# Reordering the two sides of TensorE's interleaved steps: a lone maximum first, two scores next, dense halves from the second pair

## The chip, the cores and the metric

The kernel runs on one core of one Trainium2 chip. The metric is the device time in microseconds of one launch. Differences are taken against the kernel before, whose median over three runs is 1616.48 us.

## What is computed

The input `x` has 2048 rows of 512. It is normalised row by row, and two branches read the result. One is attention with 32 heads of width 16 that share one key and one value head. The other is a dense layer to 1792, the Mish activation, and a dense layer back to 512. The second branch goes through SiLU and gates the first, and `x` is added:

```
xn = layernorm(x)
q = xn @ wq   (32 heads of 16);  k = xn @ wk;  v = xn @ wv   (one head of 16)
s = softmax(q k^T / 4) v, heads joined, @ wo
h = xn @ w1 + b1;  g = silu((h * tanh(softplus(h))) @ w2)
out = x + s * g
```

## The kernel before, in words

The attention is cut into 32 units `v` (a block of 512 queries and four heads) of 16 steps `s`, which makes 512 steps. In one step TensorE produces:

- four score tiles (`e`, line 875), each 128 keys by 512 queries, contracted over 64 rows of the array. ScalarE turns each into `pt` with an exponential (line 877). Score tiles rotate through three PSUM banks.
- four maximum tiles (`m`, line 895), which are the scores of a later unit with queries in the partitions. VectorE reduces each to its row maximum (line 899), from which the softmax shift of that unit is made. They rotate through three other banks.
- four pairs of value products (`pv`, line 949) of the step before the last. They use all 128 rows of the array, with four outputs side by side, and they close the step.
- some dense work (`xps`, line 109): a share of one of the matmul groups of the projections and of the dense branch, in the single bank that is left for it.

**Halves and pairs.** A matmul that contracts over 64 rows uses half of the array, so two of them on different halves run side by side. A score or maximum tile is such a matmul by nature. A dense matmul contracts over 128 rows and is cut into two halves that add into the same bank. In step `s`, the dense side is the row half `h = s % 2` and the other is the score side. `waves` builds both lists and issues them alternately, one dense-side matmul and one score-side matmul at a time. A chunk of `k` dense matmuls has its first halves in one step and its second halves in the next, since `h` alternates. `XMAX = 8` is the largest chunk. A group of 12 dense matmuls makes two chunks of six and so four steps. A group of 15 makes a chunk of eight and one of seven. Here these are called six-half, seven-half and eight-half steps. Counted along the trace, the stretch in which `waves` runs holds 358 six-half steps, 58 of each of the others, and 12 steps without dense work.

**Who gets the maxima.** `m_sides(1 - h, k // 2)` gives the score side `n` of the four maxima, so that both sides come out about equally long: three in six- and seven-half steps, four in eight-half steps. What is left, one lone maximum in six- and seven-half steps, goes to the dense side. `EM = "MEMEMEME"` is the order of the score side; a letter for a maximum that the side doesn't have is skipped. In a six-half step the order before is therefore, pair by pair and dense side first: x|M, x|E, x|M, x|E, x|M, x|E, M|E.

**Two waits of a dense chunk.** The second halves must not run into the bank ahead of the first ones. `waves` therefore remembers, as `relay`, the consumer of the first score-side tile that is issued after the last half (an exponential on ScalarE or a reduction on VectorE), and makes the first half of the next step wait for it. In the last step of a group no relay is needed: the group's `post` is issued right after the last half. It reads the bank out ("evacuates" it) on ScalarE (`hb` line 652 for the first dense layer, `qf` line 593 for the query projection, `y` line 717 for the first third of the second dense layer) or on VectorE (`y` lines 721 and 153, for the other two thirds and the output projection). The next group's first half waits for this evacuation, as there is one bank. For a group that VectorE evacuates, maxima that are issued between the last half but one and the last one are put on VectorE's queue behind the evacuation (`HOLD`, `held`).

The order of instructions on each engine is what this program order says: each engine works through its own queue in order. Waits of second order (buffer reuse) are inserted by the framework. Where an instruction needs two waits, one of them becomes an instruction of its own in front of it.

At the end of each step come the jobs of the activation chain on ScalarE (`act_jobs`, at most one or two), then the value products. The steps of the beginning are laid out by a planner and those of the end by `fill`; neither uses the lines that the change touches.

Of the kernel before, what the change touches and what calls it, by code (L numbers as in the profile page):

```python
# [41 lines left out]
STEP_US = 2.95  # L42
XMAX = 8
NPT = 14
EM = "MEMEMEME"
MLAG = 4
NHB = 3
NACT = 7
# [11 lines left out]
def m_need(v):  # L60

    return (40, 64)[v] if v < 2 else 32 * (v + 1)
# [53 lines left out]
def block_kernel(ctx: ExitStack, tc: tile.TileContext, x, wq, wk, wv, wo, w1, b1, w2, out):  # L116
# [232 lines left out]
    def act_jobs(n):  # L349
        n = (int(len(jobs) > 2) if gap[0] else n) if n < 9 else n  # L350
        gap[0] = 0
        while n > 0:
            k = next((k for k, (fn, free) in enumerate(jobs)
                      if free is None or free() is not None and free() <= step[0]), None)
            if k is None:
                return
            fn = jobs[k][0]
            del jobs[k]
            fn()
            n -= 1  # L360
            ran[0] += 1
# [84 lines left out]
    def pump():  # L446
        for tag in items:
            while arrived(tag):
                split(tag)
            load(tag)  # L450
# [14 lines left out]
    def begin():  # L465
        prepare()
        if qqueue and is_ready(qqueue[0]):
            g = qqueue.popleft()
        elif queue and is_ready(queue[0]):
            g = queue.popleft()  # L470
        else:
            n = next((n for n, g in enumerate(queue) if g.wo is None), None)
            if not n or not is_ready(queue[n]) or queue[n].m1 is None:
                return False
            g = queue[n]
            del queue[n]
        if g.start:
            g.start()
        if g.alloc:
            ps = g.alloc()  # L480
        else:
            ps = ps_x.tile([P, 512], F32, tag="x", name="xps")
        cur.update(g=g, n=0, ps=ps, chunk=[], relay=None)
        return True

    def finish():
        g = cur["g"]
        if cur["n"] < len(g.mms):
            return False
        for i in g.items:  # L490
            i.users -= 1
        cur["g"] = None
        evacs[0] += g.dve
        if lead:
            lead["post"](g, cur["ps"])
        else:
            g.post(cur["ps"])
            g.done = step[0]
        return True
# [14 lines left out]
    def chunk_size(n):  # L514
        return -(-n // -(-n // XMAX)) if n else 0

    def waves(h, em, new):

        if not cur["chunk"] and (not new or cur["g"] is None and not begin()):
            mms = []
        else:
            g = cur["g"]
            mms = cur["chunk"] or g.mms[cur["n"]:cur["n"] + chunk_size(len(g.mms) - cur["n"])]
        second = bool(cur["chunk"])
        k = len(mms)
        ms = em(k)
        a = deque(ms[1 - h])  # L530
        b = deque(ms[h])
        ps = cur["ps"]
        ends = second and cur["n"] + k == len(cur["g"].mms)
        xs = deque(mms)
        relay = None
        first = True
        done = False
        while a or b or xs:
            if xs:
                i = xs.popleft().half(ps, h)  # L540
                if first and cur["relay"] is not None:
                    tc.add_manual_dep(i.ins, cur["relay"].ins.name, mybir.DependencyInfo(
                        mybir.DependencyClass.Sync, mybir.DependencyReason.DATA), reason="other half of the bank")
                first = False
                if ends and cur["g"].dve and len(xs) == HOLD:
                    held[0] = []
                if not xs and ends:
                    cur["n"] += k
                    cur["chunk"] = []
                    finish()  # L550
                    done = True
                    for top in held[0] or ():
                        top()
                    held[0] = None
            elif b:
                b.popleft()()
            if len(a) > 1 or a and not xs:
                r = a.popleft()()
                if k and not xs and relay is None:
                    relay = r  # L560
        if k and not done:
            assert relay is not None
            cur["relay"] = relay
            if second:
                cur["n"] += k
                cur["chunk"] = []
            else:
                cur["chunk"] = mms
# [295 lines left out]
    def e_one(s, i):  # L864

        v, r = divmod(s, 16)
        if s < NS - LEAD:
            a, k, p = 1 - s % 2, r - r % 2 + i // 2, i % 2
        else:
            a, k, p = i % 2, r, i // 2  # L870
        q = qt_of[v]
        o = 64 * a
        ps, tag = (ps_m, "m") if NS - LEAD <= s and i in ((1, 3) if s < NS - 4 else (3,)) else (ps_e, "e")
        e = ps.tile([P, C], F32, tag=tag, name=f"e{s}_{i}")
        pe.matmul(e, ks[o:o + 64, P * k:P * (k + 1)], q[o:o + 64, p], start=True, stop=True)  # L875
        pt = sb.tile([P, C], F32, tag="pt", name=f"pt{s}_{i}", bufs=NPT)
        r = act.activation(pt, e, AF.Exp, scale=0.25)  # L877
        pt_of[16 * v + k, p, a] = pt
        return r
# [24 lines left out]
    def m_sides(h, n):  # L904

        ahead = m_next[h] - m_next[1 - h]
        lo = max((4 - MLAG - ahead + 1) // 2, 4 - (32 * NU - m_next[1 - h]))
        hi = min((4 + MLAG - ahead) // 2, 32 * NU - m_next[h])
        return max(min(n, hi), lo)
# [116 lines left out]
    def due(t):  # L1026
        step[0] = t
        for k in sorted(k for k in timed if k <= t):
            for fn in timed.pop(k):
                fn()  # L1030
# [85 lines left out]
    for c0, c1 in ((0, 1), (1, 2), (2, 4)):  # L1116
# [4 lines left out]
        for c in range(c0, c1):  # L1121
            xs, his = [], []
# [29 lines left out]
            if c == 0:  # L1152
                qp = task("PE", 2.8, lambda: fill(12), xs)
                xs = [qp]
# [33 lines left out]
    def best(eng):  # L1188
        found = None
        for k in plan[eng]:  # L1190
            s = k.start(T[eng])
            if s is not None and (found is None or (max(s, T[eng] + 0.1), k.prio) < (max(found[0], T[eng] + 0.1), found[1].prio)):
                found = (s, k)
        return found
# [5 lines left out]
    while True:  # L1200
# [7 lines left out]
        b = best("PE")  # L1208
# [13 lines left out]
        s, e, k = min(opts, key=lambda o: o[0])  # L1222
# [36 lines left out]
        elif k == "J":  # L1259
            tag = next((g for g in ("wq", "ws", "wb") if arrived(g) and busy[0] + E0 < s + 0.5), None)  # L1260
            n = ran[0]
# [16 lines left out]
    while left:  # L1278
        k = next(k for k in left if all(d.end is not None for d in k.deps))
# [6 lines left out]
    for s in range(NS + 2000):  # L1286
        inm = s < NS - LEAD
        if inm or cur["chunk"]:
            assert s < NS
            due(s)  # L1290
            h = s % 2

            def em(k):
                n = m_sides(1 - h, k // 2) if inm else 0
                x = deque(lambda i=i: e_one(s, i) for i in range(4))
                y = deque(lambda: m_one(1 - h) for _ in range(n))
                r = [[], []]
                for op in EM:
                    if op == "M" and y:
                        r[1 - h].append(y.popleft())  # L1300
                    elif op == "E":
                        r[1 - h].append(x.popleft())
                r[h] = [lambda: m_one(h) for _ in range(4 - n if inm else 0)]
                return r

            if s >= 2 and (s - 1) % 16 == 0 and s > 1:
                gap[0] += 1
            waves(h, em, inm)
            act_jobs(1 + (len(jobs) > 2))
            due(s + 0.5)  # L1310
            if s >= 2:
                pv(s - 2)
                if (s - 1) % 16 == 0 and s > 1:
                    o_out((s - 17) // 16)
        else:
            due(s)
            if s < NS:
                for i in range(4):
                    e_one(s, i)
                fill(4)  # L1320
            act_jobs(2 if s < NS else 100)
            if s < NS + 2:
                pv(s - 2)
                if (s - 1) % 16 == 0:
                    o_out((s - 17) // 16)
            due(s + 0.5)
            if s >= NS:
                fill(16)
        step[0] = s
        if vdone[0] < 8 * NC and min(m_next) >= m_need(vdone[0]):  # L1330
            r = c_rows(vdone[0])
            rowq.extend([r[0], r[1], lambda r=r: (r[2](), r[3]())])
            vdone[0] += 1
        if rowq and not evacs[0]:
            rowq.popleft()()
        evacs[0] = 0
        pump()
        if s > NS + 1 and not queue and cur["g"] is None and not timed and not jobs:
            break
# [12 lines left out]
```

## Time and profile before

| | us |
|---|---|
| median of three runs | 1616.48 (1615.63 to 1619.14) |
| span of the profiled execution, first to last instruction | 1612.9 |
| what lies around the span, taken as the median less the span | 3.6 |
| PE busy | 1594.2 (99%) |
| VectorE busy | 1348.5 (84%) |
| ScalarE busy | 1294.7 (80%) |
| GpSimd busy | 620.8 (38%) |

The page names no other time for the profiled execution than its span, so that row of the table is a difference. In the timeline PE lists matmuls, PEld their weight loads, DVE is VectorE and ACT is ScalarE. Times count from the start of the span. Where a line has "x4", four instructions of one group that follow each other are merged into one line, from the start of the first to the end of the last. A matmul's end is modelled by the profiler; starts are recorded.

### The profile page before, as it was taken

To read this page: it belongs to the slowest core of one execution; us is meant where nothing else is said; L and a number is where in the kernel's file an instruction comes from. 1 tells how busy PE (TensorE), PEld (TensorE's weight loads), DVE (VectorE), ACT (ScalarE), POOL (GpSimd) and SP (SyncE) were. 2 spreads that over 40 slices of the span, in tenths; PEclk is the share of its full clock that TensorE was granted. 3 is DMA by queue.
4 is the path that set the end of the run, shared out by engine and by line. 5 is a ranking of instruction groups with operands and counts; after the bars stand their busy time and mean duration, and the time that the engine had idled before them with its cause. 6 is when DMAs were issued, how large, how long until landed. Compare 5 with 4: busy or idle time off the path is not lost.

```text
span 1612.9 us, 31471 instructions
## 1 busy us (share of the span) xinstructions
PE 1594.2 (99%) x11615; PEld 851.9 (53%) x11615; DVE 1348.5 (84%) x2300; ACT 1294.7 (80%) x2490; POOL 620.8 (38%) x627
## 2 busy tenths in 40 slices
PE   8999999999999999999999999999999999999998
PEld 5455545555555555555555555555555555555534
DVE  8988888888988888888898988888889898888802
ACT  5478788788888778877988787797788878879885
POOL 3875176166265103421524133154153223315522
PEclk9999999999999999999999999999999999999999
DMA  5332133042231304212113321231241313022020
GB/s 161 145 115 64 41 122 111 15 148 83 70 114 52 109 23 153 70 31 91 52 27 111 92 75 26 91 119 38 67 135 34 113 57 96 23 73 78 21 86 26
DMA packets 72776, 127.30 MB, mean 79 GB/s; under 512 B 21488, under 2 KB 34288, under 8 KB 72112
## 3 DMA queue, kind: packets, MB, share of 16 engines
q1 hardware_dynamic: 72624, 125.30, 24.9%
q8 instruction: 92, 1.51, 0.4%
q14 instruction: 60, 0.49, 0.1%
HBM read 76.36 MB, written 27.26 MB: 64 GB/s over the span
## 4 chain that ended last, share of the span: by engine, by line
PE 95%; DVE 2%; ACT 1%; DMA 1%; issue 0%; POOL 0%; SPq 0%; DVEq 0%; ACTq 0%; POOLq 0%
PE xps L109 46%; PE pv L949 31%; PE m L895 8%; PE e L875 5%; PE xps L105 3%; DVE mb L899 1%; PE wop L105 1%; PE warm L1178 0%; PE kp L289 0%; ACT xin L194 0%; DMA xin<-in_dram 0%; DVE st L214 0%; DMA ws<-w 0%; DVE xin L240 0%; PE xp L250 0%
## 5 line engine op out<-in xcount | busy, mean ns | idle before, releaser
L899 DVE TENSOR_REDUCE mb<-m 128x1 f32<-128x512 f32 x2048 | 1272.8, 683 | 184.4 <-PE m L895 157.5
L877 ACT ACTIVATE pt<-e 128x512 f32<-128x512 f32 x2048 | 1068.4, 604 | 253.0 <-PE e L875 236.8
L895 PE MATMUL m<-ks,qt 48*128 48x512 f32 (+1 forms) x2048 | 837.4, 422 | 3.0 <-DVE mb L899 2.5
L875 PE MATMUL e<-qt,ks 64*128 64x512 f32 x2048 | 746.4, 410 | 0.0
L949 PE MATMUL pv<-pt,vaug 128*32 128x512 f32 x4096 | 545.3, 605 | 0.0
L895 PEld LDWEIGHTS m<-ks,qt 48*128 48x128 f32 (+1 forms) x2048 | 370.6, 185 | 67.2 <-DVE mb L899 35.2
L875 PEld LDWEIGHTS e<-qt,ks 64*128 64x128 f32 x2048 | 370.7, 186 | 26.3 <-ACT pt L877 19.6
L109 PE MATMUL xps<-xt,ws 64*128 64x512 f32 x1248 | 345.8, 410 | 0.4 <-POOL ws L153 0.2
L109 PEld LDWEIGHTS xps<-xt,ws 64*128 64x128 f32 x1248 | 215.2, 185 | 205.9 <-ACT pt L877 135.2
L109 PE MATMUL xps<-wbs,act 64*128 64x512 f32 x1158 | 312.9, 407 | 0.1
L109 PEld LDWEIGHTS xps<-wbs,act 64*128 64x128 f32 x1158 | 201.9, 185 | 166.8 <-ACT pt L877 101.5
L949 PEld LDWEIGHTS pv<-pt,vaug 128*32 128x32 f32 x4096 | 80.7, 108 | 141.9 <-issue 133.2
L163 POOL TENSOR_SCALAR t<-t 128x512 f32<-128x512 f32 x56 | 34.5, 616 | 278.4 <-ACT t L658 278.4
L153 POOL TENSOR_TENSOR hb<-hb,t 128x512 f32<-128x512 f32 x56 | 72.3, 1292 | 152.4 <-PE m L895 74.0
L109 PE MATMUL xps<-xt,wq 64*128 64x512 f32 x336 | 93.0, 409 | 0.0
L109 PEld LDWEIGHTS xps<-xt,wq 64*128 64x128 f32 x336 | 58.0, 185 | 55.4 <-ACT pt L877 35.2
L109 PE MATMUL xps<-wbs,ot_all 64*128 64x512 f32 x288 | 79.3, 407 | 0.0
L109 PEld LDWEIGHTS xps<-wbs,ot_all 64*128 64x128 f32 x288 | 49.5, 184 | 47.2 <-ACT pt L877 30.2
L153 POOL TENSOR_TENSOR hb<-hb,u 128x512 f32<-128x512 f32 x56 | 72.3, 1291 | 4.4
L153 POOL TENSOR_TENSOR u<-u,t 128x512 f32<-128x512 f32 x56 | 71.9, 1284 | 4.7
L153 POOL TENSOR_TENSOR act<-hb,act 128x512 fp32r<-128x512 f32 x55 | 70.9, 1289 | 4.6
L721 DVE TENSOR_TENSOR y<-xps,y 128x512 f32<-128x512 f32 x32 | 21.9, 683 | 58.0 <-PE xps L105 58.0
(116 smaller groups left out, 826.7 us busy)
## 6 DMA issues: line engine op xcount, KB each, us to landing
ws<-w SPq DMA_DIRECT2D x38, 512.0 KB
wbs<-w SPq DMA_DIRECT2D x36, 512.0 KB
qt<-qh SPq DMA_DIRECT2D x256, 32.0 KB
w<-ws SPq DMA_DIRECT2D x14, 512.0 KB
w<-wbs SPq DMA_DIRECT2D x14, 512.0 KB
wq<-wq SPq DMA_DIRECT2D x13, 512.0 KB
wbs<-wo SPq DMA_DIRECT2D x12, 512.0 KB
rawwb<-in_dram SPq DMA_DIRECT2D x20, 256.0 KB
```

Source lines behind the costliest of these rows:

```text
L105: self.pe.matmul(ps, self.lhs(), self.rhs(), start=(self.k == 0), stop=(self.k == self.tot - 1))
L109: i = self.pe.matmul(ps, self.lhs()[o], self.rhs()[o], start=(self.k == 0 and self.halves == 0), stop=(self.k == self.tot - 1 and self.hal ...
L153: eng.tensor_tensor(out=o, in0=a, in1=b, op=op)
L163: pool.tensor_scalar(o, o, lim, 0.0, op0=ALU.min, op1=ALU.max)
L721: dve.tensor_tensor(out=y, in0=ps, in1=y, op=ALU.add)
L875: pe.matmul(e, ks[o:o + 64, P * k:P * (k + 1)], q[o:o + 64, p], start=True, stop=True)
L877: r = act.activation(pt, e, AF.Exp, scale=0.25)
L895: pe.matmul(m, q[o, p, P * t:P * (t + 1)], ks[o, C * kb:C * (kb + 1)], start=True, stop=True)
L899: return dve.reduce_max(out=mb_of[v][:, kb, z:z + 1], in_=m, axis=AX.X)
L949: pe.matmul(o[32 * j:32 * j + 32], vaug[:, k], pt, start=(k == 0), stop=(k == 15))
```

## The change

In steps with six or seven dense halves three things change. The lone maximum of the dense side is issued ahead of the halves instead of behind them. The score side's order becomes E E M E M E M where it has three maxima. The halves therefore sit in pairs two to seven (or slots two to eight), and the tile that follows the last half, which becomes the relay, is a maximum. Pair by pair a six-half step becomes M|E, x|E, x|M, x|E, x|M, x|E, x|M. A seven-half step was x|M, x|E, x|M, x|E, x|M, x|E, x|E, M and becomes M|E, x|E, x|M, x|E, x|M, x|E, x, x|M. Steps with eight halves or none keep their order.

```diff
-EM = "MEMEMEME"
+EM = ("MEMEMEME", "EEMEMEM")
...
         while a or b or xs:
-            if xs:
+            if len(xs) == k > 0 and b and k < XMAX:
+                b.popleft()()
+            elif xs:
                 i = xs.popleft().half(ps, h)
...
-                for op in EM:
+                for op in EM[0 < k < XMAX and n == 3]:
                     if op == "M" and y:
                         r[1 - h].append(y.popleft())
```

## The prediction

> **What bounds the kernel now.** I read the page first, then the chain that ended last, then the timeline of single steps.
>
> ```profile
> span 1612.9 us, 31471 instructions
> ...
> PE 95%; DVE 2%; ACT 1%; DMA 1%; issue 0%; POOL 0%; SPq 0%; DVEq 0%; ACTq 0%; POOLq 0%
> ```
>
> TensorE's queue is the bound: 95% of the chain is PE. So the time is the sum of the lengths of the steps, and an edit is worth what it does to the length of a step. The next view is the timeline of matmuls for two six-half steps. The first starts at 620.96 and the second at 623.87.
>
> ```profile
> 620.96 0.49 PE L109 MATMUL xps<-xt,ws 64*128 64x512 f32 x1
> ...
> 622.48 0.47 PE L875 MATMUL e<-qt,ks 64*128 64x512 f32 x1
> 622.88 1.06 PE L949 MATMUL pv<-pt,vaug 128*32 128x512 f32 x8
> 623.87 0.49 PE L109 MATMUL xps<-xt,ws 64*128 64x512 f32 x1
> ...
> 624.21 0.39 PE L109 MATMUL xps<-xt,ws 64*128 64x512 f32 x1
> 624.22 0.40 PE L875 MATMUL e<-qt,ks 64*128 64x512 f32 x1
> ...
> 625.39 0.41 PE L875 MATMUL e<-qt,ks 64*128 64x512 f32 x1
> 625.73 1.06 PE L949 MATMUL pv<-pt,vaug 128*32 128x512 f32 x8
> 626.73 0.49 PE L109 MATMUL xps<-xt,ws 64*128 64x512 f32 x1
> ```
>
> The steps last 2.91 us (623.87 - 620.96) and 2.86 (626.73 - 623.87). The first pair takes 0.34 (624.21 - 623.87). The five pairs from the second to the seventh start 1.18 apart (625.39 - 624.21), 0.235 each. Undisturbed, the last pair would end 0.34 + 0.39 + 5 x 0.235 = 1.90 after the step's start. The last score really ends at 1.93 (625.39 + 0.41) in the short step and at 1.99 in the long one, 0.03 and 0.09 late. The value products start 0.07 before that recorded end, and the next step 1.00 after they start, so lateness of the last pair is lengthened step, one for one. Without it a step would last 2.83.
>
> The lateness comes from ScalarE. The fourth score needs the bank of the first score of its step (three banks), so its weight load waits for that exponential:
>
> ```profile
> 619.85 0.69 ACT L652 ACTIVATE hb<-xps,b1c 128x512 f32<-128x512 f32 x1
> 620.42 1.10 ACT L877 ACTIVATE pt<-e 128x512 f32<-128x512 f32 x2
> 621.79 2.07 ACT L877 ACTIVATE pt<-e 128x512 f32<-128x512 f32 x4 [0.28 <-PE e L875]
> 623.72 0.65 ACT L658 ACTIVATE t<-hb 128x512 f32<-128x512 f32 x1
> 624.65 2.06 ACT L877 ACTIVATE pt<-e 128x512 f32<-128x512 f32 x4 [0.28 <-PE e L875]
> ```
>
> ```profile
> 623.98 0.19 PEld L109 LDWEIGHTS xps<-xt,ws 64*128 64x128 f32 x1
> ...
> 625.30 0.18 PEld L875 LDWEIGHTS e<-qt,ks 64*128 64x128 f32 x1
> ```
>
> In the short step the first exponential starts at 624.65 and ends 0.60 later, at 625.25. The fourth score's load follows at 625.30, 0.05 later, and its matmul ends at 625.80, 0.50 after the load. Undisturbed, a pair's load comes much earlier: that of the second pair at 623.98, 0.62 before its matmul's end (624.60). So a load may be 0.12 late for free, and after that its matmul's end is load + 0.50. For the second pair the load may come up to 0.23 after the step's start. In the long step the first exponential starts 0.83 after the step's start (621.79) instead of 0.78, since it has a second wait in front of it:
>
> ```profile
> L877 ACTq EVENT_SEMAPHORE  x319: 17/17/17, 107.2 to 1553.6; - x160
> ```
>
> Counted along the timeline of ScalarE, 174 of the 358 six-half steps have that extra wait before their first exponential and 184 have not. Their mean lateness is (174 x 0.09 + 184 x 0.03) / 358 = 0.06, a mean step of 2.89.
>
> **The change, part by part.** Nothing is added or removed. No DMA moves and no step is passed, as only the order within a step differs. What matters is who is late next.
>
> *Two scores first.* The first score moves from pair two to pair one, the fourth from pair seven to pair six. The trace has a first pair of this kind in a step without dense work:
>
> ```profile
> 230.66 0.49 PE L875 MATMUL e<-qt,ks 64*128 64x512 f32 x1
> ...
> 231.19 1.29 DVE L899 TENSOR_REDUCE mb<-m 128x1 f32<-128x512 f32 x2 [0.22 <-PE e L875]
> 231.22 1.09 ACT L877 ACTIVATE pt<-e 128x512 f32<-128x512 f32 x2 [0.63 <-PE e L875]
> ...
> 231.94 0.18 PEld L895 LDWEIGHTS m<-ks,qt 48*128 48x128 f32 x1 [0.72 <-DVE mb L899]
> ```
>
> Its exponential starts 0.56 after the step (231.22 - 230.66). It ends at 1.16, the fourth score loads at 1.21 and ends at 1.71, against 0.34 + 0.39 + 4 x 0.235 = 1.67 undisturbed. That is 0.04 to 0.05 late, I take 0.05; the maximum behind it on the same half is as late. The extra wait disappears, as I read the code: the first score now stands ahead of the first half and has its own wait on ScalarE, which also tells the exponential that its buffer's old writer is done. In the step without dense work shown, every score has such a wait, and its exponential starts with no extra 0.05. A plain step then lasts 2.83 + 0.05 = 2.88 for 2.89: 0.01 x 358 = **3.6 us gained**.
>
> How soon an exponential follows its matmul differs by the place in these rows: 0.07 after the recorded end here (231.22 against 230.66 + 0.49), 0.03 in pair two (624.65 against 624.22 + 0.40). I go by start to start in the same place, 0.56; with recorded end and 0.03 the exponential would start at 0.52 or 0.53 and a step would be 0.03 shorter, which is rival 4. [...]
>
> *The relay becomes a maximum.* Four reductions start 0.56 after the step (621.52 - 620.96) and need 2.48 together:
>
> ```profile
> 621.52 2.48 DVE L899 TENSOR_REDUCE mb<-m 128x1 f32<-128x512 f32 x4 [0.42 <-PE m L895]
> ```
>
> The maxima keep pairs one, three, five and seven, so the last reduction ends at 3.04. From a reduction's end to a load that waits for it are 0.06 (231.19 + 0.69 to 231.94). The relay opens at 3.10, which is 0.22 in the next step, and the limit of the second pair is 0.23. Behind the first half the whole TensorE queue waits (second score, all other halves), but a delay there also covers the fourth score's 0.05. So it may come 0.06 later than computed for nothing. I take 0; beyond that it costs what it slips.
>
> *Evacuation behind four exponentials.* Now the last half comes in pair seven, behind the fourth score, so ScalarE evacuates after four exponentials instead of two or three. Queued behind it are the next step's exponentials, and TensorE's first half waits for it.
>
> ```profile
> L652 ACT ACTIVATE hb<-xps,b1c 128x512 f32<-128x512 f32 x56 | 38.7, 692 | 8.0 <-PE xps L105 8.0
> ...
> L717 ACT ACTIVATE y<-xps 128x512 f32<-128x512 f32 x16 | 9.8, 611 | 0.0
> ...
> L593 ACT ACTIVATE qf<-xps 128x512 f32<-128x512 f32 x15 | 9.0, 603 | 4.8 <-PE xps L105 4.8
> ```
>
> Four exponentials take 2.07, so their starts are 0.49 apart. The evacuation starts at 0.56 + 3 x 0.49 + 0.48 = 2.51. `hb` ends at 3.20 and opens the load at 3.25, which is 0.37 in the next step. In a six-half step that is 0.14 over the limit, and since it covers the 0.05 there, **0.09 net**. `qf` and `y` (0.08 shorter) stay within that 0.05: nothing. An eight-half step starts with a half, whose load has no slack at all: 0.37 after `hb`, 0.28 after `qf`, and 0.12 after `y`, which closes a seven-half step (3.04, rows below) and ends at 3.12. I counted the successors along the trace: 39 `hb` to six halves, 3.5 us; to eight halves four `hb`, five `qf`, nine `y`, 1.5 + 1.4 + 1.1 = 4.0 us. Before, the evacuation at 619.85 ended at 620.54, ahead of the next step (620.96), so all of it is new: **7.5 us lost**.
>
> [...]
>
> *VectorE's evacuation.* In a six-half group's last step it now takes the fourth place on VectorE, ending at 3.04, in time as the relay is. The fourth maximum follows, 0.60 behind, so the next step's reductions start at 0.68 instead of 0.56, 0.12 late. Their relay is then 0.06 beyond its margin: 0.06 x 24 such successions, **1.4 us lost**.
>
> ```profile
> 606.25 0.49 PE L109 MATMUL xps<-wbs,act 64*128 64x512 f32 x1
> ...
> 609.29 0.50 PE L109 MATMUL xps<-xt,ws 64*128 64x512 f32 x1
> ```
>
> A seven-half step, as this one, lasts 3.04, so relay and fourth score stay hidden in it; its lone slot passes from a maximum to a half. Nothing gained or lost.
>
> Sum: -3.6 + 7.5 + 1.4 = +5.3 us on a span of 1612.9, that is 1618.2; with the 3.6 around it 1621.8, and as much on the median of 1616.48.
>
> **The rivals.**
>
> 1. *Extra waits stay.* If as many first exponentials as now keep their second wait, 174 x 0.05 = 9 us come on top: 1631. Against it: the step without dense work above, whose scores carry their own waits.
> 2. *The relay binds.* If reductions end 0.10 later than computed, the relay passes its margin by 0.04 in every second step (the longer step gives the next one room), 180 x 0.04 = 7 us: 1629. It decides from 0.06 on. Against it: the quoted 2.48, which repeats from step to step.
> 3. *The late evacuation is hidden*, the rival on the other side. If TensorE's first halves wait for something that comes later anyway (weights from GpSimd, buffers), the 7.5 us fall to about 3: 1617, no change. It decides where a weight comes 0.23 into a step or later. Against it: the two steps above start with no such wait.
> 4. *Faster.* With the first exponential at 0.53 the fourth score is 0.02 late and a plain step lasts 2.85, 0.03 x 358 = 11 us less: 1611. The relay (0.25 in) still passes, by the 0.02 that it covers; the evacuations come 0.03 earlier in steps that are 0.03 shorter, the same loss. Three hundredths of latency decide, so it has weight.
> [...]
>
> That the change does nothing can't be: six- and seven-half steps are 416 of 486.
>
> **How the numbers follow.** Forecast as summed 0.53, rival 1 0.11, rival 2 0.06, rival 3 0.12, rival 4 0.16, rival 5 0.02: 1.00 together. A difference of 0.2% (3.2 us) is about what can be told from none. Faster by more than that is most of rival 4, 0.14. Within it lie the rest of rival 4, rival 3 and the low end of the forecast, together 0.20. Slower: 0.66. The range goes from rival 4, 1611, to rival 1, 1632 with rounding; within it lies what latencies of 0.02 in 358 steps (7 us) leave open about the forecast, and rival 5 and the far ends of 2 and 4 are left out.
>
> **What would show it.**
>
> ```profile
> PEld xps L109 <- ACT hb L652: 30.2, 36, 0.8
> ```
>
> Right: this line of the waits rises above 36 waits and above 0.8 us for the longest. The extra waits on ScalarE's queue, 319, fall below 150, plain six-half steps lie at 2.88, and eight-half steps behind a ScalarE evacuation grow by 0.1 to 0.4. Wrong: plain steps at 2.85 (rival 4) or 2.93 (rival 1), or reductions (`mb`) as the last releaser of first halves together with steps above 2.90 (rival 2). A time under 1613 would mean that the plain step was mis-sized, a time above 1632 that the order of ScalarE's queue costs more than one load.

## The result and the profile after

The changed kernel takes 1622.1 us (median of 5 runs, 1621.19 to 1623.95), the kernel before in the same measurement 1615.63 us (5 runs, 1614.38 to 1619.14). The ratio is 1.0039, 95% interval 1.0026 to 1.0052: slower by 6.5 us. The forecast was 1621.8 in a range of 1611 to 1632.

One correction to the bookkeeping: the runs measured now list time and span together, and 1.8 us lie around the span (1622.10 and 1620.3), not 3.6. The profile of before came from a run that was faster than its median. So the forecast span of 1618.2 is 2.1 us short of the measured 1620.3, and 1.8 us of the forecast's 1621.8 came from a wrong remainder, which hides most of that. From profile to profile the change costs 7.4 us (1620.3 - 1612.9).

Head and chain of the page after:

```profile
span 1620.3 us, 31269 instructions
...
PE 93%; ACT 4%; DVE 2%; issue 1%; DMA 0%; SPq 0%; ACTq 0%; DVEq 0%
```

TensorE still carries the chain, but ScalarE's share rises from 1% to 4%. There are 202 instructions fewer: 167 fewer waits in front of exponentials, 39 fewer waits on TensorE's queue of weight loads, and four more waits elsewhere. Next, the timeline of a plain six-half step after the change, from 748.98 to 751.84, the lines of ScalarE, VectorE and the weight loads that could be late:

```profile
748.98 0.18 PEld L897 LDWEIGHTS m<-ks,qt 48*128 48x128 f32 x1 [0.84 <-DVE mb L901]
...
749.51 2.48 DVE L901 TENSOR_REDUCE mb<-m 128x1 f32<-128x512 f32 x4 [0.41 <-PE e L877]
749.55 2.06 ACT L879 ACTIVATE pt<-e 128x512 f32<-128x512 f32 x4 [0.83 <-PE e L877]
...
750.20 0.18 PEld L877 LDWEIGHTS e<-qt,ks 64*128 64x128 f32 x1
...
750.26 0.43 PE L877 MATMUL e<-qt,ks 64*128 64x512 f32 x1
...
751.84 0.18 PEld L897 LDWEIGHTS m<-ks,qt 48*128 48x128 f32 x1 [0.84 <-DVE mb L901]
...
752.05 0.18 PEld L109 LDWEIGHTS xps<-xt,ws 64*128 64x128 f32 x1
```

The first exponential starts 0.57 after the step (749.55 - 748.98) and, 0.60 long, ends at 750.15. The fourth score's load follows at 750.20, 1.22 into the step. The reductions end at 751.99 (749.51 + 2.48), and the first half of the next step loads at 752.05, 0.21 into that step. This step lasts 2.86; the median of the plain ones is 2.875.

Two six-half steps after the change, the first ending with ScalarE's evacuation:

```profile
633.36 2.06 ACT L879 ACTIVATE pt<-e 128x512 f32<-128x512 f32 x4 [0.20 <-PE e L877]
...
635.28 0.71 ACT L654 ACTIVATE hb<-xps,b1c 128x512 f32<-128x512 f32 x1
635.65 0.18 PEld L897 LDWEIGHTS m<-ks,qt 48*128 48x128 f32 x1 [0.84 <-DVE mb L901]
636.04 0.18 PEld L109 LDWEIGHTS xps<-xt,wq 64*128 64x128 f32 x1 [0.21 <-ACT hb L654]
...
638.64 0.18 PEld L897 LDWEIGHTS m<-ks,qt 48*128 48x128 f32 x1 [0.84 <-DVE mb L901]
```

`hb` starts behind four exponentials, ends at 635.99, and the next step's first half loads at 636.04, 0.39 after that step began at 635.65. That step lasts 2.99 (638.64 - 635.65). Where an eight-half step follows, the half stands first and the whole wait counts; here behind `qf`:

```profile
1020.39 1.06 PE L951 MATMUL pv<-pt,vaug 128*32 128x512 f32 x8
1021.00 0.63 ACT L595 ACTIVATE qf<-xps 128x512 f32<-128x512 f32 x1
1021.68 0.18 PEld L109 LDWEIGHTS xps<-wbs,act 64*128 64x128 f32 x1 [1.14 <-ACT qf L595]
```

The load comes 1.29 after the value products start (1021.68 - 1020.39) instead of 1.00. The line of the waits that the prediction named, and two of its neighbours:

```profile
PEld xps L109 <- ACT pt L879: 23.5, 28, 0.8
...
PEld xps L109 <- ACT hb L654: 11.5, 37, 1.2
PEld xps L109 <- ACT y L719: 8.6, 9, 1.0
```

This line has to be read with care. Its total falls, from 30.2 to 11.5, while its cost rises. Before, its 36 waits were mostly the 0.84 in which every step's first load stands idle while value products run, which cost nothing. Now 33 of its 37 are waits of some 0.2 inside a step, which do cost, and four are of 1.2, 0.4 above the free 0.84.

From the loads of all steps I sorted the steps by their own kind and by what the step ahead ended with. A length goes from first load to first load; a wait between the value products and a first load is booked to the step that it delays. Mean lengths in us:

| kind of step | steps | before | after | total |
|---|---|---|---|---|
| six halves, plain | 238 | 2.886 | 2.882 | -1.0 |
| six halves, behind `hb` | 39 | 2.951 | 3.015 | +2.5 |
| six halves, behind `qf` or `y` | 15 | 2.917 | 2.904 | -0.2 |
| six halves, one or two steps behind VectorE's evacuation | 58 | 2.893 | 2.891 | -0.1 |
| six halves, right behind a step without dense work | 6 | 3.102 | 3.508 | +2.4 |
| seven halves | 58 | 3.054 | 3.057 | +0.2 |
| eight halves, behind `hb`, `qf` or `y` | 18 | 3.107 | 3.340 | +4.2 |
| other eight halves | 40 | 3.110 | 3.095 | -0.6 |

They add up to the 7.4 us. Behind `hb`, `qf` and `y` the eight-half steps grow by 0.38, 0.33 and 0.11 each (forecast 0.37, 0.28 and 0.12). The fifth row was not in the forecast. The timeline of such a step after the change:

```profile
795.30 0.87 PE L897 MATMUL m<-ks,qt 48*128 48x512 f32 x3
795.67 0.18 PEld L897 LDWEIGHTS m<-ks,qt 48*128 48x128 f32 x1 [0.18 <-DVE mb L901]
...
796.58 0.18 PEld L897 LDWEIGHTS m<-ks,qt 48*128 48x128 f32 x1 [0.62 <-DVE mb L901]
796.58 0.50 PE L897 MATMUL m<-ks,qt 48*128 48x512 f32 x1 [0.18 <-DVE mb L901]
```

A step without dense work leaves its neighbour with several maxima on the dense side, and the first edit puts all of them in front: maxima follow each other with only three banks for them, and a load stands 0.62 waiting for a reduction.

### The profile page after: what moved, and what is told of

Its sections match the earlier page's. It is cut to its first block, busy times and chain, and to the rows that moved or that the text cites. A ratio compares the mean times of both kernels' runs of the same rounds, so it can differ in the third digit from the quotient of the medians.

```text
span 1620.3 us, 31269 instructions
## 1 busy us (share of the span) xinstructions
PE 1597.8 (99%) x11615; PEld 839.8 (52%) x11615; DVE 1350.5 (83%) x2300; ACT 1292.8 (80%) x2490; POOL 620.6 (38%) x627
## 4 chain that ended last, share of the span: by engine, by line
PE 93%; ACT 4%; DVE 2%; issue 1%; DMA 0%; SPq 0%; ACTq 0%; DVEq 0%
PE xps L109 32%; PE pv L951 30%; PE m L897 18%; PE e L877 8%; PE xps L105 3%; ACT pt L879 2%; DVE mb L901 1%; PE wop L105 1%; PE warm L1180 0%; PE kp L289 0%; ACT xin L194 0%; ACT y L719 0%; DMA xin<-in_dram 0%; DVE st L214 0%; ACT hb L654 0%
## 5 line engine op out<-in xcount | busy, mean ns | idle before, releaser
L877 PE MATMUL e<-qt,ks 64*128 64x512 f32 x2048 | 789.3, 431 | 0.3 <-ACT pt L879 0.3
L877 PEld LDWEIGHTS e<-qt,ks 64*128 64x128 f32 x2048 | 358.1, 184 | 29.8 <-ACT pt L879 18.0
L109 PE MATMUL xps<-xt,ws 64*128 64x512 f32 x1248 | 328.9, 395 | 0.0
L109 PE MATMUL xps<-wbs,act 64*128 64x512 f32 x1158 | 303.1, 398 | 2.8 <-ACT hb L654 1.2
L109 PEld LDWEIGHTS xps<-wbs,act 64*128 64x128 f32 x1158 | 207.8, 185 | 76.7 <-ACT pt L879 23.5
L109 PEld LDWEIGHTS xps<-xt,ws 64*128 64x128 f32 x1248 | 222.7, 184 | 29.1 <-ACT hb L654 4.8
L109 PE MATMUL xps<-xt,wq 64*128 64x512 f32 x336 | 88.1, 394 | 0.0
L109 PE MATMUL xps<-wbs,ot_all 64*128 64x512 f32 x288 | 75.1, 393 | 0.0
L153 POOL TENSOR_TENSOR oc<-oc,sc 128x512 f32<-128x512 f32 (+1 forms) x16 | 20.6, 1286 | 123.3 <-ACT sc L979 123.3
```

The lines of the kernel that those rows point to most:

```text
L109: i = self.pe.matmul(ps, self.lhs()[o], self.rhs()[o], start=(self.k == 0 and self.halves == 0), stop=(self.k == self.tot - 1 and self.hal ...
L153: eng.tensor_tensor(out=o, in0=a, in1=b, op=op)
```

## The experiments

**The evacuation put ahead of the fourth exponential.** The evacuation's place on ScalarE is the term that decided the forecast's sign. This kernel is the changed one with one queue order altered:

```diff
+        if hold:
+            late.append(top)      # top() issues the exponential
+            return None
...
+                hold = k in (6, 7) and bool(cur["chunk"]) and cur["n"] + k == len(g.mms) and not g.dve
...
             waves(h, em, inm)
+            while late:
+                late.pop(0)()
```

> The changed kernel, but in the last step of a group that ScalarE evacuates (six or seven halves) the fourth score's exponential is issued behind the evacuation; its matmul stays where it is. Theory (the late evacuation is what the change costs): ScalarE starts the evacuation 0.49 us earlier, hb ends at about 2.75 in its step instead of 3.20, and the next first half no longer waits for it. By the changed kernel's steps that returns 39 x 0.13 where a six-half step follows hb and about 4.2 us where an eight-half step follows hb, qf or y: some 9 us, 1613. Rival 3 (first halves wait for weights or relays anyway): nothing, 1621 to 1623. Rival (the plain step with its fourth score in pair six is what costs): nothing either, and plain steps stay at 2.875 in both cases.

Measured: 1614.98 us (12 runs) beside 1615.54 for the kernel before (21 runs), ratio 0.9993, interval 0.9983 to 1.0004. So 7 us of the change's cost are gone. Expected were some 9, and 1613. The rows of the table behind a ScalarE evacuation do give back 8.9 us against the changed kernel in the profiles; but one early step, the one treated under "Both repairs together", is 1.2 longer than there, and the first step in which `waves` issues dense work ends 2.9 us later (100.79 for 97.91). The same succession as above, in this kernel:

```profile
633.88 1.57 ACT L884 ACTIVATE pt<-e 128x512 f32<-128x512 f32 x3 [0.20 <-PE e L879]
...
635.33 0.70 ACT L654 ACTIVATE hb<-xps,b1c 128x512 f32<-128x512 f32 x1
635.90 0.62 ACT L884 ACTIVATE pt<-e 128x512 f32<-128x512 f32 x1
636.19 0.18 PEld L904 LDWEIGHTS m<-ks,qt 48*128 48x128 f32 x1 [0.84 <-DVE mb L908]
636.30 0.19 PEld L109 LDWEIGHTS xps<-xt,wq 64*128 64x128 f32 x1
```

`hb` now ends at 636.03, ahead of the step at 636.19, and the half loads 0.11 into the step with no wait. It also shows on the line of the waits, where only the four waits of 0.84 that cost nothing are left:

```profile
PEld xps L109 <- ACT hb L654: 3.4, 4, 0.8
```

Six-half steps behind `hb` fall to 2.906 (median 2.874), eight-half steps behind `hb` and `qf` to 3.174 and 3.111, as long as before. Rival 3, by which first halves wait for something else anyway, falls. The kernel says something of rival 2 as well: steps behind `hb`, whose first half comes 0.11 into the step, have a median of 2.874, and plain steps, whose first half waits for the relay until about 0.20, one of 2.875. So the relay is not what sets a plain step.

**Only a lone maximum first.** The unforecast row, taken out of the changed kernel by one condition:

```diff
-            if len(xs) == k > 0 and b and k < XMAX:
+            if len(xs) == k > 0 and len(b) == 1 and k < XMAX:
```

> The changed kernel, but a maximum of the dense side goes first only where it is the last one there; steps whose dense side still has three maxima put their halves first again. Theory: only the six-half steps right behind a step without dense work change (three or so of them, 3.63 us instead of 3.1), so 1.5 to 2.4 us less: about 1620. Rival (those steps are long for the change of TensorE's order, whatever goes first): no change. No other step should move.

Measured: 1620.43 us (10 runs), ratio to before 1.0031, interval 1.0022 to 1.0040. The six steps' mean goes from 3.508 to 3.107 (3.102 before the change), 2.4 us together, and every other row of the table stays within 0.3 us of the changed kernel's. The theory holds by the steps; the two kernels' times alone do not tell them apart, as the interval of the changed kernel (1.0026 to 1.0052) overlaps this one. Five steps, not three, had been long.

**Each edit alone.** Each of these two was run once, since both were expected to be far off:

```diff
-EM = ("MEMEMEME", "EEMEMEM")
+EM = ("MEMEMEME", "MEMEMEME")
```

> The first edit alone: the dense side's lone maximum goes first, the score side keeps its old order (maximum first). Theory (three banks for maxima): pair one now holds two maxima, the fourth maximum comes in pair five and waits for the first one's reduction, which ends at 1.23; its load at 1.28 and its matmul's end at 1.78 are 0.34 behind the undisturbed 1.435, so a six-half step lasts about 3.17 and a seven-half step 0.3 more too: 358 x 0.30 + 58 x 0.3 + a few for evacuations = about 1750. Rival (each edit acts for itself, and the lone maximum in front costs only the order of the relay): within 10 us of the changed kernel.

and, the other way round, with the new `EM` kept:

```diff
-            if len(xs) == k > 0 and b and k < XMAX:
-                b.popleft()()
-            elif xs:
+            if xs:
```

> The second edit alone: the score side begins with two scores, the dense side puts its halves first and its lone maximum last, as before. Theory: pair seven holds two maxima, and the fourth waits for the reduction of the first of its step, which comes only in pair three and ends at about 1.69; load 1.74, matmul's end 2.24 for 1.90, so a six-half step lasts about 3.17, a seven-half step 0.1 longer: 358 x 0.30 + 58 x 0.1 = some 110 us, about 1730. The relay (an exponential that ends at 2.6) costs nothing, and the extra waits in front of first exponentials stay as many as before. Rival (the second edit is the harmful one through its evacuation, the first edit is neutral): about 1620.

Measured: 1725.1 us for the first edit alone and 1736.6 us for the second alone, beside 1615.54 before and 1622.1 for both together. A step of the first edit alone:

```profile
789.53 0.50 PE L897 MATMUL m<-ks,qt 48*128 48x512 f32 x2
789.88 0.19 PEld L897 LDWEIGHTS m<-ks,qt 48*128 48x128 f32 x1
790.06 2.48 DVE L901 TENSOR_REDUCE mb<-m 128x1 f32<-128x512 f32 x4 [0.67 <-PE m L897]
...
790.81 0.18 PEld L897 LDWEIGHTS m<-ks,qt 48*128 48x128 f32 x1 [0.28 <-DVE mb L901]
```

The fourth maximum loads 1.28 after the step (790.81 - 789.53), as computed, and plain steps last 3.17. With the second edit alone it loads at 1.78 (computed: 1.74), in the step from 790.50 after a wait of 0.17 for a reduction, and they last 3.20. My sum for the first edit alone was 25 us too high. About 10 of that are the seven-half steps, which grew by 0.12 and not by 0.3; that their eighth slot gives room is my guess, which no run shows by itself. The two edits are one edit. Either alone brings the maxima too close together for three banks, and only both keep them in pairs one, three, five and seven.

**Both repairs together.**

> The changed kernel with both repairs: the fourth exponential behind ScalarE's evacuation in a group's last step, and a dense maximum first only where it is a lone one. Theory (the costs stand in different steps and add up): hold4's steps together were as long as before's (-0.1 us) with 3.7 us still lost in the steps behind those without dense work, so 3.8 us under the kernel before: about 1611.7, with plain steps still at 2.875. Rival (long steps only move: what is taken out here comes back as a wait elsewhere): as hold4, 1615.

Measured: 1614.35 us (11 runs), ratio 0.9992, interval 0.9984 to 1.0001. That isn't shown to be faster than before, and 2.7 us above what I expected. The repaired steps are as expected: five of the six behind a step without dense work are back to their old lengths (3.10 to 3.29, one at 2.88), and no other row moved. But the sixth, early in the kernel, lasts 4.51, with the exponentials queued behind a ScalarE job that waits for GpSimd:

```profile
238.78 0.63 ACT L660 ACTIVATE t<-hb 128x512 f32<-128x512 f32 x1 [1.76 <-POOL hb L153]
```

The same step takes 4.07 to 4.88 in the profiles of two other kernels here (the evacuation ahead, and the next one) and 3.12 to 3.15 in the profile of the lone maximum and in that of before. The granted clock of the beginning may have a part in it: over the first 70 us it was 0.95 in the three profiles with the long step, and 1.00 in those of before, of the changed kernel (3.64) and of the lone maximum. But it was 0.95 for the second edit alone too, where the step lasts 3.11, so the cause stays open. In this profile the clock fell a second time, to 0.61 from 90.0 to 97.8 and 0.56 from 97.8 to 102.5, where it is 1.00 in the profile of before; the first step in which `waves` issues dense work ended 4.6 us later (102.49 against 97.89). On the page the third slice shows it:

```profile
PEclk9989999999999999999999999999999999999999
```

The single runs agree: those with a mean granted clock of 0.999 and more took 1611.45 to 1611.73 us, those at 0.993 and 0.994 took 1616.9. The kernel before, in the same measurement, took 1613.41 to 1615.61 at 0.999 and more, so at an equal clock this kernel looks some 3 us faster. That grouping was made after the fact, and whether the kernel itself brings the lower clock about is open. So the two costs are separate and add up in their steps; the time of the whole is blurred by a few us that lie ahead of them.

**The extra wait, taken by itself.** The change's one gain was forecast from the extra wait in front of first exponentials. This kernel is the one before, in its old order, and each fourth exponential gets a dependency on the fourth exponential of the step before:

```diff
+        if i == 3:
+            if last4[0] is not None:
+                tc.add_manual_dep(r.ins, last4[0].ins.name, mybir.DependencyInfo(
+                    mybir.DependencyClass.Sync, mybir.DependencyReason.DATA), reason="buffers of the next four")
+            last4[0] = r
         return r
```

> The kernel before, in its old order, with one dependency added: each fourth exponential waits for the fourth exponential of the step before (long done), so that ScalarE is known to be past the old writers of the next buffers. As built, the waits of their own in front of exponentials fall from 319 to 18, none of them in front of a first exponential of a step. Theory (the extra wait is why 174 of the 358 plain steps last 2.905 and not 2.85): all plain steps come to 2.85, 174 x 0.055 = 9 us less, about 1606. Rival (long and short steps differ by something else, such as where the weights lie or which half of the bank goes first): no change, 1615.5, with two kinds of steps as now. Should the added wait cost as much in front of the fourth exponential, the relay or the evacuation behind it slips by 0.05 and part of the gain is lost.

Measured: 1605.39 us (5 runs, 1603.19 to 1605.77) beside 1614.98 for the kernel before (15 runs), ratio 0.9933, interval 0.9920 to 0.9947. The waits in front of its exponentials, and the timeline of two plain steps (the first is the one from 620.96 in the profile of before):

```profile
L879 ACTq EVENT_SEMAPHORE  x18: 17/17/17, 1520.3 to 1575.2; - x18
```

```profile
619.58 0.18 PEld L109 LDWEIGHTS xps<-xt,ws 64*128 64x128 f32 x1 [0.84 <-ACT hb L652]
620.36 2.07 ACT L879 ACTIVATE pt<-e 128x512 f32<-128x512 f32 x4 [0.21 <-PE e L877]
...
622.43 0.18 PEld L109 LDWEIGHTS xps<-xt,ws 64*128 64x128 f32 x1 [0.84 <-ACT pt L879]
623.21 2.06 ACT L879 ACTIVATE pt<-e 128x512 f32<-128x512 f32 x4 [0.27 <-PE e L877]
...
625.28 0.18 PEld L109 LDWEIGHTS xps<-xt,ws 64*128 64x128 f32 x1 [0.84 <-ACT pt L879]
```

The first exponentials start 0.78 after both steps, where the step from 620.96 had 0.83, and both steps last 2.85. Of the 356 six-half steps in the table 258 now lie between 2.84 and 2.86, where before 124 did and 132 lay between 2.90 and 2.92. The steps together are 10.3 us shorter. The added wait costs nothing visible in front of the fourth exponential, where ScalarE has work queued anyway: the four take 2.07 and 2.06 in these rows, as in those of before. Besides the waits in front of exponentials, 27 waits at line 658, a job of the activation chain, are gone as well. But before, plain steps with a second wait in front of their first exponential had a median of 2.91 and the others of 2.85, and now all have one of 2.85, so it is this wait that counts. It is the fastest kernel of this study, in the old order of the step.

## Why the prediction was right

The sign and the mechanism held. That 1621.8 came within 0.3 us of 1622.1 is luck. In the span 2.4 us were missing because six-half steps gained less than forecast, and another 2.4 in steps that the sum left out; 2.7 us of other terms came out lower (1.5 at VectorE's evacuation, 0.8 at ScalarE's, 0.4 in seven-half and the other eight-half steps). The 2.1 us that remain were nearly made up by the 1.8 us too much around the span. Term by term:

- *A plain step at 2.88 for 2.89, -3.6 us.* After: 2.882, median 2.875. First exponential at 0.57 (forecast 0.56), fourth load at 1.22 (1.21). Before: 2.886, since its short steps last 2.85 and not 2.86. So the gain per step was 0.004 and not 0.01, and plain steps brought only -1.0, with those behind `qf` and `y` -1.2. The difference of 0.01, taken between two means that were known no better than that, was mis-sized.
- *Extra waits.* Forecast: below 150. The waits in front of the exponentials of the changed kernel:

```profile
L879 ACTq EVENT_SEMAPHORE  x152: 17/17/17, 108.0 to 1561.1; - x152
```

  152 of 319 are left. By the waits of the two programs as built, those in front of a step's first exponential fell from 245 to 35, and in six- and seven-half steps from 210 to none; most of the rest, 116, stand in front of a third one, where ScalarE has work queued anyway (in the six-half steps after the change a third exponential starts 0.48 behind the second, with such a wait and without). The mechanism held, the bound was two too low, and the last experiment shows it alone at work. Rival 1 falls.
- *The relay, 0.* Right: the first half loads 0.19 into a plain step (median; 0.21 in the row above), and steps without that wait are no shorter (2.874).
- *ScalarE's evacuation, +7.5.* +6.7 in the rows behind `hb`, `qf` and `y` that grew. In the rows above `hb` ends 0.34 into the next step and opens the load at 0.39; forecast were 0.32 and 0.37. The eight-half steps cost 4.2 (forecast 4.0). The six-half steps behind `hb` cost 2.5 (3.5): their mean was 2.951 before, not 2.89, since some (3.02 to 3.34) were already held up, mostly by a ScalarE job behind the evacuation, and those hardly grow.
- *VectorE's evacuation, +1.4.* Nothing: -0.1 over 58 steps. The 24 steps in question, the second ones behind such an evacuation, do last 2.911, 0.04 over a plain one, with their first half at 0.31; but before the change the same steps lasted 2.903. So the cost is less than the 0.06 I computed, and little of it is new, because these steps were longer than plain ones before too; why they were was not looked into.
- *Not in the sum.* +2.4 in steps behind those without dense work, where the first edit moves several maxima. I had read the condition in the code only for a lone one.

The price curve held throughout: a first half at 0.20, 0.31 and 0.39 into the step goes with 2.875, 2.911 and 2.99; computed are 2.88 up to the limit, and beyond it 2.83 plus what lies over 0.23, which gives 2.91 and 2.99. Rival 2 falls with the relay's row and rival 4 with the 0.57. Rival 5, which has 0.02 of the chances, is exponentials end to end. No run shows such a thing: four exponentials of 128x512, 0.60 each, take 2.06 in the rows above, where end to end they would take 2.40.

So the change won what it could win in the plain step, about 1 us of the 10 that the extra waits are worth, because its new order spends the rest on a fourth score that comes one pair earlier (plain steps of 2.875, where the old order without the extra waits has 2.85); and it then paid for an evacuation that had been free.

## What to carry to other kernels

ScalarE took its instructions in program order here: in the two rows of `hb` above it started 0.37 ahead of the next step behind four exponentials (635.28 against 635.65) and 0.86 ahead of it behind three (635.33 against 636.19). So ask of every instruction that is moved ahead what it now stands in front of: a score one pair earlier and a last half one pair later put four exponentials before an evacuation, and 57 steps waited for it. Look at the waits before the order: one redundant wait in front of the first exponential, moved to where the engine was busy anyway, was worth more (10 us) than the 3.6 us that the reordering was forecast to gain. And a total on a line of waits says little by itself: here that of `hb` fell by 19 us while its cost rose by 4, since waits under running work had been counted and the new ones lay in the open.

## What the runs showed of the hardware

A second wait in front of an exponential costs about 0.06 us where ScalarE is idle for it, in both places where the runs have it. In pair two it delays the first exponential by 0.05 in the two steps of the prediction (0.83 against 0.78), and by 0.06 in the medians of the plain steps before the change (0.84 against 0.78). With the second edit alone the first score stands in pair one and often keeps its second wait. The timeline of that kernel shows a first exponential without it, from 816.67, and one with it, from 819.94:

```profile
816.14 0.50 PE L875 MATMUL e<-qt,ks 64*128 64x512 f32 x1
...
816.67 2.06 ACT L877 ACTIVATE pt<-e 128x512 f32<-128x512 f32 x4 [1.14 <-PE e L875]
...
819.34 0.49 PE L875 MATMUL e<-qt,ks 64*128 64x512 f32 x1
...
819.94 1.57 ACT L877 ACTIVATE pt<-e 128x512 f32<-128x512 f32 x3 [0.60 <-PE e L875]
```

They start 0.53 and 0.60 after their matmuls start; the medians over the plain steps are 0.54 and 0.60. Where ScalarE has work queued, no price is visible: in the six-half steps of the changed kernel the third exponential starts 0.478 behind the second where a second wait stands in front of it (median of 54 steps) and 0.477 where none does (305 steps).

The delay from a matmul's recorded end to the exponential isn't set by the pair. It is 0.03 in pair two before the change and 0.03 in pair one here (816.67 against 816.14 + 0.50), but 0.07 in pair one of the prediction's step without dense work, and in the changed kernel the first exponential starts at 0.57. In the first two cases the partner on the other half of the array is a dense half, in the last two a maximum. Whether that is the reason was not tested. Carrying the start-to-start distance from a pair of the same make-up was what worked (0.56 forecast, 0.57 measured).
